# Soft-capped attention with a spectral mix: the second pair's scores of the mixing slots move next to the first pair's

## The chip, the cores and the metric

The kernel runs on one core of one Trainium2 chip. The metric is the device time of one execution in microseconds (us). Three runs of the kernel before took 862.06, 863.33 and 863.35 us; their median is 863.33 us. One further execution was profiled.

## What is computed

Eight batches, twelve heads, 448 tokens, head size 64; the attention's output feeds a mix over tokens and over 768 features.

```python
scores = scale * q @ k.T                    # per batch and head
scores = cap * tanh(scores / cap)
attn = exp(scores - max); attn = attn / (sum(attn) + 1e-09)
x = (attn @ v) as [8, 448, 768]
theta = x @ w_theta
zr, zi = x * cos(theta), x * sin(theta)
y = einsum('ts,bsd->btd', w_tok_r, zr) + einsum('ts,bsd->btd', w_tok_i, zi)
u = x + y
out = u + maximum(u @ w_ch, 0)
```

## The kernel before

Heads are taken in pairs (64 + 64 rows fill the 128 partitions), and two pairs at a time make a **slot** `s`: 24 slots, three for each batch. A slot makes the transposed scores of its two pairs, tanh and exp on them, and the column sums; the product with `v` (`V0`, `W`, `Vr`), the reciprocal (`I`) and the scaling (`N`, two multiplications on VectorE) of slot `s` come during slot `s + 1`. The queries and keys are split into a high and a low float32r part (`prep_q`, `prep_k`), so a score block takes three matmuls, each as two matmuls of 64 rows side by side. The 448 keys are three blocks of 128 and a rest of 64.

From slot 4 on, each slot also carries one third of the spectral mix of an earlier batch, and that is its part, `(s - 4) % 3`: part 0 makes theta (`T`, turns `y`, reduction `d`, sine and cosine `sc`, product with x `r`, a 32 x 32 transpose `f`, and a carry `D` that moves the blocks by 16 DMAs), part 1 is the **mixing slot** (slots 5, 8, 11, 14, 17, 20, 23), part 2 makes the channel product (`C`, `c`, splits `u` and `X`). In a mixing slot the six features j = 0 to 5 (of 128 columns each) are mixed over the 896 token rows (cosine and sine). A feature comes in two halves, a (four blocks, 512 wide in the rows of the profile) and b (three blocks, 384 wide). `h2a` is the high part of feature 2's half a: a cast on ScalarE (L647). `l2a` is its low part: a subtraction on VectorE (L654). `M2a` is its matmuls (three for each block, L664 to L666; the third of each block reads the low part). `m2` adds the result to x on VectorE (L672). Two features share one carried tile: `f0`, `f1` and `D0` bring features 0 and 1, `f2`, `f3` and `D1` features 2 and 3, `f4`, `f5`, `D2` and `E2` features 4 and 5. `E2` is the last four of the sixteen pieces, issued on ScalarE's queue (L633).

What each engine does, and in which order, is written out by hand: `PARTS` has one string of words for each part, `OTHER` the strings of single slots, and `run` issues the words from left to right. Each engine executes its own share in that order, and so do the queues that issue DMAs. The word `S0` makes two key blocks of the first pair, `S1` the third block and both pairs' rests, `S2` and `S3` the second pair's; `t0` to `t3` are their tanhs and `e0` to `e3` their exps (on ScalarE), `a0a` ... `a1b` add the exps of a pair on VectorE (L435, L438, L439), `F0` and `F1` fold the sums (transpose L446, reduce L447), and `Rb` has TensorE sum the folds (L487), which it takes in order. `Pa1`, `Pb1` split query and key of the slot's second pair, `Pa0` and `Pb0` those of the next slot's first.

`once(s)` is true for slots whose scores come in two visits of TensorE: `S0` by itself, and `S1`, `S2`, `S3` one after the other. In these slots `S2` writes two banks of the pool `psM`, `S3` writes the score bank that held the rests and two more banks of `psM`. There are four `psM` banks, and the mix, theta and channel sums take them too. Before, `once` holds for parts 0 and 2 from slot 9 on:

```python
    ONCE = (0, 2)
    def once(s):
        return s > LEAD + 3 and s < NS and (s - LEAD) % NP2 in ONCE
```

Of the kernel before, what the change touches and what calls it, by code (L numbers as in the profile page):

```python
# [12 lines left out]
F32 = mybir.dt.float32  # L13
# [15 lines left out]
LEAD = 4  # L29
# [53 lines left out]
def softcap_attn_then_spectral_mix(ctx, tc, qk2, v, cap, w_theta, w_tok, w_ch, outT):  # L83
# [200 lines left out]
            state["scores"] = state["scope"].enter_context(tc.tile_pool(name=f"ps{general}{s}", bufs=1, space=bass.MemoryType.PSUM))  # L284

    def once(s):
        return s > LEAD + 3 and s < NS and (s - LEAD) % NP2 in ONCE

    def load_raw(k, part, last=False):
        t = raw[k, part] = small.take([P, S], F32, f"{'qk'[part]}{k}", None, int(part == 0 and once(k // 2) and (k // 2 - LEAD) % NP2 == 2), last)  # L290
        nc.sync.dma_start(t, qk2[k // NP, k % NP, :, part, :])
# [19 lines left out]
            if once(k // 2) and k % 2 and (k // 2 - LEAD) % NP2:  # L311
                Q[k, "rooms"] = [small.take([P, S], F32R, f"k{k}{part}") for part in "hl"]

    def prep_k(k):

        if 2 * WHOLE <= k < 2 * NS:
            t = raw.pop((k, 1))
            if once(k // 2) and k % 2:
                if (k, "rooms") not in Q:
                    Q[k, "rooms"] = [small.take([P, S], F32R, f"k{k}{part}") for part in "hl"]  # L320
                rooms = iter(Q[k, "rooms"])
                Q[k, "k"] = halves(t[:, :REST], [P, REST], lambda shape, dtype, name: next(rooms)[:, :REST], f"k{k}", by_scalar(k))
# [55 lines left out]
    def direct(s):  # L378
        return state["general"] or s < DIRECT

    def tanh(s, n):
        m = len(BURSTS[n])
        if m == 2:
            pp = large.take([P, 2, 2, S], F32, f"p{s}_{n}", EXPS if s < LEAD - 1 else None, s >= LEAD and n != 2)
            users[s, n] = [pp, {0: {"V0"}, 1: {"Vr", "V0"}, 2: {"W"}}[n] | (({"Ra", "Rb"}, {"Ra"}, {"Ra", "Rb"})[n] if direct(s) else set())]
        else:
            pp = wk.tile([P, 1, 2, S], F32, tag="p1", name=f"p{s}_{n}", bufs=1)
        for u, what in enumerate(BURSTS[n]):
            U[s, what] = pp[:, u]
        t, whole = spt.pop((s, n)) if not isinstance(spt[s, n], list) else (spt.pop((s, n)), None)  # L390
# [286 lines left out]
    def chan_out(b, m):  # L677
# [15 lines left out]
    )  # L693
    OTHER = {
# [19 lines left out]
    def pipeline(general):  # L714
        state["general"] = general
        nc.scalar.activation(curve, quarter, AF.Tanh)
        def run(s, b, word):
# [9 lines left out]
                scores(s + 1, 0)  # L727
            elif name in ("S", "t", "e"):
                if live:
                    {"S": scores, "t": tanh, "e": exp}[name](s, i)  # L730
            elif not name:
                if live:
                    add(s, i, half)
# [33 lines left out]
            elif name == "q":  # L767
                for part in range(2):
                    if s + 1 < WHOLE or s + 1 == WHOLE and (i, part) != (1, 1):
                        load_raw(2 * s + 2 + i, part)  # L770
            elif word == "Pa1":
                prep_q(2 * s + 1)
            elif word == "Pb1":
                prep_k(2 * s + 1)
# [94 lines left out]
```

## Time and profile before

| what | us |
|---|---|
| median of 3 runs (862.06 to 863.35) | 863.33 |
| the profiled execution, its own time | 861.66 |
| span of the profiled execution | 859.5 |
| TensorE matmuls busy | 852.2 (99%) |
| VectorE busy | 714.9 (83%) |
| ScalarE busy | 582.4 (68%) |
| GpSimd busy | 111.1 (13%) |

The span runs from the first to the last instruction that the profile shows; 2.16 us of the execution lie around it. The granted clock of TensorE is 0.999 of full speed. Busy time of TensorE counts overlapping matmuls once and their ends are modelled, so steps between the starts of matmuls tell more than their durations. VectorE and ScalarE start an instruction up to 0.1 us before the row of the one ahead of it ends, so chains there are added up from start to start.

### The profile page before, as it was taken

Reading aid. Unit: us, or ns where it says so; the run is one execution under the profiler, and the core shown is the slowest. Engines: PE = TensorE matmul, PEld = TensorE weight load, DVE = VectorE, ACT = ScalarE, POOL = GpSimd, SP = SyncE. Lnnn points to the kernel's source line nnn. Section 1 sums busy time; section 2 is a strip of 40 time slices with the busy share of each in tenths; the row PEclk is TensorE's granted clock in tenths of the full one; section 3 lists DMA queues with packets and bytes.
Section 4 is the critical chain, followed back from the end, with each engine's and each line's share of the span. In section 5 each row is a group of like instructions: output and inputs, shape, how many; then the busy total and the mean of one; then the engine's idle time right before and its main releaser. Section 6 shows DMA issues by size and latency. Waiting matters only on the chain.

```text
span 859.5 us, 13319 instructions
## 1 busy us (share of the span) xinstructions
PE 852.2 (99%) x4756; PEld 645.8 (75%) x4756; DVE 714.9 (83%) x1153; ACT 582.4 (68%) x734; POOL 111.1 (13%) x232
## 2 busy tenths in 40 slices
PE   9999999999999999999999999999999999999997
PEld 4335676867878778778787787797787977879996
DVE  5988989999799798989979798897879979776741
ACT  7898987769783777827968479655778377824420
POOL 1121242201300031000310013000130003100300
PEclk9999999999999999999999999999999999999999
DMA  8686275731522334331523314133152332311501
GB/s 315 189 304 229 75 239 196 249 108 53 152 73 90 96 88 121 87 104 54 139 78 97 125 49 132 50 119 118 44 140 68 101 101 74 99 43 31 143 13 56
DMA packets 51884, 99.74 MB, mean 116 GB/s; under 512 B 11232, under 2 KB 42592, under 8 KB 51808
## 3 DMA queue, kind: packets, MB, share of 16 engines
q1 hardware_dynamic: 38304, 58.13, 21.7%
q0 software_dynamic: 9184, 29.20, 11.0%
q10 hardware_dynamic: 4320, 11.47, 4.5%
q8 instruction: 39, 0.64, 0.3%
q14 instruction: 37, 0.30, 0.1%
HBM read 54.72 MB, written 11.01 MB: 76 GB/s over the span
## 4 chain that ended last, share of the span: by engine, by line
PE 96%; ACT 2%; DMA 1%; SPq 1%; issue 0%; POOL 0%; DVE 0%; ACTq 0%; POOLq 0%
PE s L376 13%; PE a L473 13%; PE mx L664 8%; PE mx L666 7%; PE mx L665 7%; PE th L563 7%; PE ch L563 7%; PE ch L564 7%; PE ch L565 7%; PE th L564 7%; PE th L565 7%; PE a L467 2%; PE r L508 2%; PE s_u L376 1%; ACT p L396 1%; DMA t<-g_row 1%
## 5 line engine op out<-in xcount | busy, mean ns | idle before, releaser
L633 POOL DMA_DIRECT2D t<-g_row x148 | 73.5, 504 | 538.1 <-ACT z L587 381.1
L664 PE MATMUL mx<-wtk_h,zh 128*128 128x448 f32 x336 | 125.1, 372 | 0.0
L666 PE MATMUL mx<-wtk_h,zl 128*128 128x448 f32 x336 | 123.7, 368 | 0.1
L665 PE MATMUL mx<-wtk_l,zh 128*128 128x448 f32 x336 | 123.5, 367 | 0.0
L415 ACT ACTIVATE p<-p,singles 128x1792 f32<-128x1792 f32 (+1 forms) x76 | 117.7, 1556 | 1.7 <-PE a L473 0.6
L563 PE MATMUL th<-xs,wth_h 128*128 128x448 f32 x288 | 106.2, 369 | 0.0
L563 PE MATMUL ch<-us,wch_h 128*128 128x448 f32 x288 | 106.0, 368 | 0.0
L564 PE MATMUL ch<-us,wch_h 128*128 128x448 f32 x288 | 105.6, 367 | 0.0
L565 PE MATMUL ch<-us,wch_l 128*128 128x448 f32 x288 | 105.6, 367 | 0.0
L564 PE MATMUL th<-xs,wth_h 128*128 128x448 f32 x288 | 105.5, 366 | 0.0
L565 PE MATMUL th<-xs,wth_l 128*128 128x448 f32 x288 | 105.5, 366 | 0.0
L402 ACT ACTIVATE p<-s,singles 128x896 f32<-128x896 f32 x48 | 45.7, 1004 | 85.4 <-PE s L376 85.3
L473 PE MATMUL a<-p,v 128*64 128x448 f32 x492 | 101.8, 545 | 0.0
L654 DVE TENSOR_TENSOR zl<-t,zh 128x512 fp32r<-128x512 f32 x88 | 52.9, 618 | 28.7 <-ACT zh L647 23.7
L473 PEld LDWEIGHTS a<-p,v 128*64 128x64 f32 x492 | 32.9, 137 | 56.5 <-issue 51.7
L647 ACT CAST zh<-t 128x512 fp32r<-128x512 f32 x88 | 46.9, 563 | 37.3 <-DMA t<-g_row 12.9
L664 PEld LDWEIGHTS mx<-wtk_h,zh 128*128 128x128 f32 x336 | 63.1, 188 | 11.6 <-issue 5.0
L666 PEld LDWEIGHTS mx<-wtk_h,zl 128*128 128x128 f32 x336 | 63.1, 188 | 6.5 <-DVE zl L654 0.9
L665 PEld LDWEIGHTS mx<-wtk_l,zh 128*128 128x128 f32 x336 | 63.2, 188 | 5.5
L563 PEld LDWEIGHTS th<-xs,wth_h 128*128 128x128 f32 x288 | 54.1, 188 | 8.1 <-issue 1.6
L563 PEld LDWEIGHTS ch<-us,wch_h 128*128 128x128 f32 x288 | 54.1, 188 | 6.9 <-ACT p L399 1.6
L564 PEld LDWEIGHTS th<-xs,wth_h 128*128 128x128 f32 x288 | 54.0, 188 | 4.9 <-DVE xs L556 0.2
(673 smaller groups left out, 1690.3 us busy)
## 6 DMA issues: line engine op xcount, KB each, us to landing
v<-in_v ACTq DMA_DIRECT2D x22, 448.0 KB, 3.9
bc<-ri SPq DMA_DIRECT2D x76, 112.0 KB, 2.9
t<-g_row SPq DMA_DIRECT2D x148, 56.0 KB, 2.4
t<-g_row POOLq DMA_DIRECT2D x148, 56.0 KB, 2.3
out_dram<-x SPq DMA_DIRECT2D x36, 224.0 KB, 1.9
q<-in_qk SPq DMA_DIRECT2D x35, 224.0 KB, 2.9
k<-in_qk SPq DMA_DIRECT2D x34, 224.0 KB, 3.8
x_row<-in_qk SPq DMA_DIRECT2D x27, 224.0 KB, 3.4
```

The costliest lines, as they stand in the source:

```text
L376: nc.tensor.matmul(out[h][rows, :S], kk[half], qq[half], start=m == 0, stop=m == len(products) - 1)
L415: nc.scalar.activation(pp, pp, AF.Exp, scale=cap_sb)
L473: nc.tensor.matmul(acc_of["a", s, i][h * D : (h + 1) * D, :S], vt[s][:, 6 * i + 3 * h + c, :], U[s, (i, c)][:, h, :], start=first and c == ...
L563: nc.tensor.matmul(acc[:, :S], wh[:, j, ms], t[:, 0, :], start=j == 0, stop=False)
L564: nc.tensor.matmul(acc[:, :S], wh[:, j, ms], t[:, 1, :], start=False, stop=False)
L565: nc.tensor.matmul(acc[:, :S], wl[:, j, ms], t[:, 0, :], start=False, stop=j == NJ - 1)
L633: queue.dma_start(t[32 * m : 32 * m + 32, d * S : (d + 1) * S], f[32 * d : 32 * d + 32, m * S : (m + 1) * S])
L647: nc.scalar.copy(zh.rearrange("p c (d x) -> p c d x", x=32), tokens(b, j)[:, c0:c1])
L654: nc.vector.tensor_tensor(zl, tokens(b, j)[:, c0:c1], zh.bitcast(F32), op=ALU.subtract)
L664: nc.tensor.matmul(acc[:, :S], zh, wtk_h[:, c, :], start=c == 0, stop=False)
L665: nc.tensor.matmul(acc[:, :S], zh, wtk_l[:, c, :], start=False, stop=False)
L666: nc.tensor.matmul(acc[:, :S], zl, wtk_h[:, c, :], start=False, stop=c == NC2 - 1)
```

## The change

`once` now holds for every slot from 9 to 23, so the mixing slots 11, 14, 17, 20 and 23 make their scores in two visits as well. The strings of part 0 and part 1 are written anew for that; slot 8 keeps the old string of a mixing slot under a name of its own, with an `N` more. The core of the diff:

```diff
-ONCE = (0, 2)
...
     def once(s):
-        return s > LEAD + 3 and s < NS and (s - LEAD) % NP2 in ONCE
+        return LEAD + 4 < s < NS
...
-    def tanh(s, n):
+    def tanh(s, n, part=""):
...
         if once(s) and n == 3:
-            nc.scalar.activation(pp[:, 0], spt.pop((s, "u"))[:, :, :S], AF.Tanh, scale=qscale)
-            for h, each in enumerate(t):
-                nc.scalar.activation(U[s, (1, 1)][:, h], each[:, :S], AF.Tanh, scale=qscale)
+            if part != "a":
+                nc.scalar.activation(pp[:, 0], spt.pop((s, "u"))[:, :, :S], AF.Tanh, scale=qscale)
+            if part != "b":
+                for h, each in enumerate(spt.pop((s, n))):
+                    nc.scalar.activation(U[s, (1, 1)][:, h], each[:, :S], AF.Tanh, scale=qscale)
+            return
...
-        if j < 4 or not 0 < b < B - 1:
+        if j < 4 or not 0 < b < B - 1 or once(LEAD + NP2 * b + 1):
             nc.vector.tensor_scalar(y.bitcast(I32), n.bitcast(I32), 0x7FFFFFFF, None, op0=ALU.bitwise_and)
...
     PARTS = (
-        "S0 t0 V0 e0 Pa1 W Ra Rb Vr cV0 S1 Pb1 cV1 t1 S2 S3 v w0 q0 I w1 a0a Pa0 Pb0 q1 t2 e1 a0b T0 y0 t3 N d0 e2 F0 T1 y1 e3 d1 a1a sc0 a1b T2 y2 r0 r1 f0 f1 D0 T3 y3 d2"
-        " d3 T4 y4 sc1 F1 T5 y5 r2 r3 f2 f3 D1",
-        "S0 t0 V0 h0a l0a h0b l0b W h1a Ra Rb Vr cV0 cV1 d4 d5 l1a Pa1 S1 t1 sc2 Pb1 q0 M0a h1b sc2b l1b I M0b r4 r5 h2a m0 l2a f4 f5 D2 M1a e0 M1b e1 h2b l2b w1 h3a E2"
-        " S2 S3 m1 M2a l3a M2b h3b l3b t3 a0a M3a h4a l4a M3b h4b l4b t2 a0b m2 v q1 M4a h5a e2 l5a m3 M4b"
-        " h5b l5b Pa0 Pb0 F0 e3 a1a M5a m4 M5b a1b w3 m5 F1",
+        "S0 t0 V0 e0 Pa1 Pb1* W Ra Rb Vr cV0 S1 cV1 t1 S2 S3 v w0 q0 I w1 a0a Pa0 Pb0 q1 t2 Pa3 e1 a0b T0 y0 t3 N d0 e2 F0 Pb3* T1 y1 e3 d1 a1a sc0 a1b T2 y2 r0 r1 f0 f1 D0 T3 y3 d2"
+        " d3 T4 y4 d4 sc1 F1 T5 y5 r2 r3",
+        "S0 t0 V0 f2 W Ra Rb f3 D1 h0a Vr cV0 S1 cV1 t1a S2 S3 t2 l0a h0b d5 l0b I h1a l1a sc2b M0a h1b M0b r4 l1b r5 h2a M1a t3a f4 l2a h2b f5 D2 m0 l2b M1b h3a w1 E2 t1b"
+        " N M2a h3b l3a l3b m1 M2b e0 t3b a0a M3a h4a l4a e1 M3b h4b l4b h5a l5a a0b e2 M4a m2 F0 e3 m3 M4b h5b l5b v q1 Pa0 Pb0 a1a M5a m4 M5b a1b w3 m5 F1",
```

A tanh word with a or b after it does half of its work; `Pa3` and `Pb3*` split query and key of the next slot's second pair; a star keeps the raw key until `S1`. Part 2 and the string after the last slot lose an `N-` (the scaling of the slot before the last), which the mixing slot now does by its own `N`. In slot 8 the `N` stands between `m3` and `M4b`. `cV1`, the copy of the second pair's product, goes from ScalarE to VectorE in the mixing slots, and so does the absolute value of theta's last two features.

**TensorE, slot 11, from the third block of the first pair on.** `s11_10` is that block, `s11_20` to `s11_31` and `s11_u` are the second pair's, `mx2_0` is feature 0. Before:

```order
L376 MATMUL s11_10_2951<-q22h_2670,k22l_2675 128x448 x2
L376 MATMUL s11_10_2951<-q22l_2671,k22h_2674 128x448 x2
L664 MATMUL mx2_0_2974<-wtk_h_75,zh2_2917 128x448
L665 MATMUL mx2_0_2974<-wtk_l_76,zh2_2917 128x448
L666 MATMUL mx2_0_2974<-wtk_h_75,zl2_2918 128x448
```

and with the change:

```order
L379 MATMUL s11_u_2976<-q23l_2686,k23h_2689 128x448 x2
L379 MATMUL s11_u_2976<-q23h_2685,k23l_2690 128x448 x2
L379 MATMUL s11_30_2974<-q23h_2685,k23h_2689 128x448
L379 MATMUL s11_31_2975<-q23h_2685,k23h_2689 128x448
L379 MATMUL s11_30_2974<-q23l_2686,k23h_2689 128x448
L379 MATMUL s11_31_2975<-q23l_2686,k23h_2689 128x448
L379 MATMUL s11_30_2974<-q23h_2685,k23l_2690 128x448
L379 MATMUL s11_31_2975<-q23h_2685,k23l_2690 128x448
L674 MATMUL mx2_0_3011<-wtk_h_75,zh2_2942 128x448
L675 MATMUL mx2_0_3011<-wtk_l_76,zh2_2942 128x448
L676 MATMUL mx2_0_3011<-wtk_h_75,zl2_2943 128x448
```

The nine pairs of the second pair's scores, which stood between feature 1 and feature 2, now stand ahead of feature 0.

**ScalarE, slot 11, around the four carry DMAs of `E2`.** `zh2` from `t2_1` and `t2_2` are the high parts of features 2, 3 and 4, 5 (512 is half a, 384 half b); an ACTIVATE at L402 or L399 (L411, L401, L398 in the change) is a tanh, one at L415 (L425) an exp, and `g_row_79` holds the exps' second tile. Before:

```order
L415 ACTIVATE p11_0_2907<-p11_0_2907,singles_64 128x1792
L415 ACTIVATE g_row_79<-g_row_79,singles_64 128x1792
L647 CAST zh2_2917<-t2_1_2876 128x384
L647 CAST zh2_2917<-t2_1_2876 128x512
L633 DMA t2_2_3018<-g_row_79 32x448 x4
L647 CAST zh2_2917<-t2_1_2876 128x384
L399 ACTIVATE p11_3_3110<-s11_30_3076,singles_64 128x448
L399 ACTIVATE p11_3_3110<-s11_31_3077,singles_64 128x448
L647 CAST zh2_2917<-t2_2_3018 128x512
L647 CAST zh2_2917<-t2_2_3018 128x384
```

and with the change:

```order
L657 CAST zh2_2942<-t2_1_2925 128x384
L657 CAST zh2_2942<-t2_1_2925 128x512
L643 DMA t2_2_3058<-g_row_79 32x448 x4
L411 ACTIVATE g_row_79<-s11_10_2918,singles_64 128x896
L657 CAST zh2_2942<-t2_1_2925 128x384
L425 ACTIVATE p11_0_2900<-p11_0_2900,singles_64 128x1792
L398 ACTIVATE p11_3_3051<-s11_u_2976,singles_64 128x896
L657 CAST zh2_2942<-t2_2_3058 128x512
L425 ACTIVATE g_row_79<-g_row_79,singles_64 128x1792
L657 CAST zh2_2942<-t2_2_3058 128x384
L657 CAST zh2_2942<-t2_2_3058 128x512
```

The two exps `e0` and `e1` stood ahead of the four DMAs and now stand behind them, with a tanh ahead of the first.

**VectorE, slot 11, the low parts of features 4 and 5** (`zl2` from `t2_2`), with the additions and the fold of the first pair's exps (`ps11_0`, `ft11_0`) and the sums of features 2 and 3 (`mx2_2`, `mx2_3`). Before:

```order
L654 TENSOR_TENSOR zl2_2918<-t2_2_3018,zh2_2917 128x512
L654 TENSOR_TENSOR zl2_2918<-t2_2_3018,zh2_2917 128x384
L438 TENSOR_TENSOR ps11_0_3113<-ps11_0_3113,g_row_79 128x896
L439 TENSOR_TENSOR ps11_0_3113<-ps11_0_3113,g_row_79 64x896
L672 TENSOR_TENSOR x7_0_1979<-mx2_2_3085,x7_0_1979 128x448
L654 TENSOR_TENSOR zl2_2918<-t2_2_3018,zh2_2917 128x512
L672 TENSOR_TENSOR x7_1_1981<-mx2_3_3115,x7_1_1981 128x448
L654 TENSOR_TENSOR zl2_2918<-t2_2_3018,zh2_2917 128x384
L301 TENSOR_TENSOR q24l_3178<-x_row_80,q24h_3177 128x448
L301 TENSOR_TENSOR k24l_3182<-k24_2972,k24h_3181 128x384
L327 COPY r24_3185<-k24_2972 128x64
L446 STREAM_TRANSPOSE ft11_0_3189<-ps11_0_3113 128x896
```

and with the change:

```order
L664 TENSOR_TENSOR zl2_2943<-t2_2_3058,zh2_2942 128x512
L664 TENSOR_TENSOR zl2_2943<-t2_2_3058,zh2_2942 128x384
L664 TENSOR_TENSOR zl2_2943<-t2_2_3058,zh2_2942 128x512
L448 TENSOR_TENSOR ps11_0_3118<-ps11_0_3118,g_row_79 128x896
L449 TENSOR_TENSOR ps11_0_3118<-ps11_0_3118,g_row_79 64x896
L682 TENSOR_TENSOR x7_0_1979<-mx2_2_3090,x7_0_1979 128x448
L456 STREAM_TRANSPOSE ft11_0_3166<-ps11_0_3118 128x896
L457 TENSOR_REDUCE folds_78<-ft11_0_3166 128x28
L682 TENSOR_TENSOR x7_1_1981<-mx2_3_3120,x7_1_1981 128x448
L664 TENSOR_TENSOR zl2_2943<-t2_2_3058,zh2_2942 128x384
L299 TENSOR_TENSOR q24l_3185<-x_row_80,q24h_3184 128x448
```

Feature 5's half a moved ahead of the addition; its half b, which stood ahead of the fold, now stands behind it.

## Rows read from the trace of the kernel before

**Rows 1.** The page, chain that ended last: shares of the span by engine

```profile
PE 96%; ACT 2%; DMA 1%; SPq 1%; issue 0%; POOL 0%; DVE 0%; ACTq 0%; POOLq 0%
```

**Rows 2.** Windows: slots 17 and 20, from `S0` to `S0`; length, then busy by engine

```profile
513.99:550.81 36.82, 36.82 (x208) 29.10 (x208) 31.75 (x49) 29.46 (x38) 8.40 (x17) 1.00 0.40 116
616.19:653.51 37.32, 37.26 (x209) 28.91 (x208) 30.44 (x47) 29.46 (x38) 8.53 (x17) 1.00 0.41 115
```

**Rows 3.** Timeline of PE, slot 17: start, duration, engine, line, operation, count

```profile
520.97 0.54 PE L376 MATMUL s<-q,r 64*64 64x448 f32 x1
...
532.97 0.37 PE L376 MATMUL s<-q35l,k35h 64*128 64x448 f32 x2
533.26 0.47 PE L664 MATMUL mx<-wtk_h,zh 128*128 128x448 f32 x1
533.57 0.36 PE L665 MATMUL mx<-wtk_l,zh 128*128 128x448 f32 x1
533.77 0.36 PE L666 MATMUL mx<-wtk_h,zl 128*128 128x448 f32 x1
```

**Rows 4.** Timeline of PE, slot 16 (part 0), its second visit

```profile
488.33 0.54 PE L376 MATMUL s<-q,r 64*64 64x448 f32 x1
...
491.84 0.47 PE L563 MATMUL th<-xs,wth_h 128*128 128x448 f32 x1
```

**Rows 5.** Timeline of ACT and its DMA queue, slot 17; in brackets idle before, releaser

```profile
525.21 1.28 ACT L604 ACT_TABLE_LOAD   x1
526.51 1.05 ACT L604 ACTIVATE z<-z,singles 128x896 f32<-128x896 f32 x1
...
533.70 1.18 ACTq L633 DMA_DIRECT2D t<-g_row  x2
...
534.92 1.26 ACTq L633 DMA_DIRECT2D t<-g_row  x2
536.27 0.51 ACT L647 CAST zh<-t 128x384 fp32r<-128x384 f32 x1 [0.84 <-ACT zh L647]
536.69 1.16 ACT L399 ACTIVATE p<-s,singles 128x448 f32<-128x448 f32 x2
539.74 0.62 ACT L647 CAST zh<-t 128x512 fp32r<-128x512 f32 x1 [1.89 <-PE mx L666]
...
540.67 1.90 ACT L402 ACTIVATE p<-s,singles 128x896 f32<-128x896 f32 x2
542.47 0.61 ACT L647 CAST zh<-t 128x512 fp32r<-128x512 f32 x1
542.98 1.80 ACT L415 ACTIVATE p<-p,singles 128x1792 f32<-128x1792 f32 x1
```

**Rows 6.** Timeline of DVE, slot 17

```profile
528.43 1.09 DVE L609 TENSOR_TENSOR z<-z,x 128x896 f32<-128x896 f32 x1 [0.59 <-ACT z L605]
529.44 1.08 DVE L609 TENSOR_TENSOR z<-z,x_row 128x896 f32<-128x896 f32 x1
...
531.57 2.10 DVE L617 STREAM_TRANSPOSE g_row<-z 128x896 f32<-128x896 f32 x2
...
541.46 1.08 DVE L438 TENSOR_TENSOR ps<-ps,g_row 128x896 f32<-128x896 f32 x1
...
543.59 0.61 DVE L672 TENSOR_TENSOR x<-mx,x 128x448 f32<-128x448 f32 x1
544.12 0.67 DVE L654 TENSOR_TENSOR zl<-t,zh 128x512 fp32r<-128x512 f32 x1
...
545.26 0.54 DVE L654 TENSOR_TENSOR zl<-t,zh 128x384 fp32r<-128x384 f32 x1
...
546.83 1.09 DVE L446 STREAM_TRANSPOSE ft<-ps 128x896 f32<-128x896 f32 x1
```

**Rows 7.** Timeline of DVE, then of PE, start of slot 9, behind slot 8

```profile
248.75 1.09 DVE L447 TENSOR_REDUCE folds<-ft 128x28 f32<-128x896 f32 x1
...
249.66 0.53 PE L487 MATMUL s<-folds,diagonal 128*64 128x28 f32 x4
```

More of the change, by code (lines that the diff above doesn't have):

```diff
@@ L312, in prep_q, with prep_k @@
                 Q[k, "rooms"] = [small.take([P, S], F32R, f"k{k}{part}") for part in "hl"]
-    def prep_k(k):
+    def prep_k(k, early=False):
         if 2 * WHOLE <= k < 2 * NS:
-            t = raw.pop((k, 1))
+            t = raw[k, 1]
             if once(k // 2) and k % 2:
@@ L327, in prep_k @@
                 nc.vector.tensor_copy(Q[k, "r"], t[:, REST:])
-            small.give(t)
+            if early:
+                Q[k, "early"] = True
+            else:
+                small.give(raw.pop((k, 1)))
             if k + 1 < 2 * NS:
@@ L357, in scores @@
                     small.give(raw.pop((k + i, 0)))
+                if Q.pop((k + 1, "early"), False):
+                    small.give(raw.pop((k + 1, 1)))
                 if k + 2 < 2 * NS:
-                    load_raw(k + 2, 0)
-                    load_raw(k + 3, 0)
+                    for i in range(2, 4):
+                        load_raw(k + i, 0, once(s) and (s - LEAD) % NP2 == 2)
     def chunk(s, what, out):
@@ L379, in direct @@
         return state["general"] or s < DIRECT
-    def tanh(s, n):
+    def tanh(s, n, part=""):
         m = len(BURSTS[n])
[L383 to L390, printed above, removed]
-        if once(s) and n == 3:
-            nc.scalar.activation(pp[:, 0], spt.pop((s, "u"))[:, :, :S], AF.Tanh, scale=qscale)
-            for h, each in enumerate(t):
-                nc.scalar.activation(U[s, (1, 1)][:, h], each[:, :S], AF.Tanh, scale=qscale)
-        elif whole is not None:
+        if part != "b":
+            if m == 2:
+                pp = large.take([P, 2, 2, S], F32, f"p{s}_{n}", EXPS if s < LEAD - 1 else None, s >= LEAD and n != 2)
+                users[s, n] = [pp, {0: {"V0"}, 1: {"Vr", "V0"}, 2: {"W"}}[n] | (({"Ra", "Rb"}, {"Ra"}, {"Ra", "Rb"})[n] if direct(s) else set())]
+            else:
+                pp = wk.tile([P, 1, 2, S], F32, tag="p1", name=f"p{s}_{n}", bufs=1)
+            for u, what in enumerate(BURSTS[n]):
+                U[s, what] = pp[:, u]
+            U[s, "t", n] = pp
+        pp = U[s, "t", n]
+        if once(s) and n == 3:
+            if part != "a":
+                nc.scalar.activation(pp[:, 0], spt.pop((s, "u"))[:, :, :S], AF.Tanh, scale=qscale)
+            if part != "b":
+                for h, each in enumerate(spt.pop((s, n))):
+                    nc.scalar.activation(U[s, (1, 1)][:, h], each[:, :S], AF.Tanh, scale=qscale)
+            return
+        t, whole = spt[s, n] if isinstance(spt[s, n], tuple) else (spt[s, n], None)
+        if whole is not None:
             nc.scalar.activation(pp, whole[:, :m, :, :S], AF.Tanh, scale=qscale)
@@ L400, in tanh @@
         else:
-            for u in (1, 0) if n == 1 else range(m):
+            for u in {"a": (1,), "b": (0,)}.get(part, (1, 0) if n == 1 else range(m)):
                 nc.scalar.activation(pp[:, u], t[u][:, :, :S], AF.Tanh, scale=qscale)
-        U[s, "t", n] = pp
+        if part != "a":
+            del spt[s, n]
     def used(s, word):
@@ L476, in av_out @@
     def av_out(s, i):
-        x = small.take([P, S], F32, f"x{s}_{i}")
+        x = small.take([P, S], F32, f"x{s}_{i}", None, int(i == 1 and once(s + 1)))
         (nc.vector.tensor_copy if i and once(s + 1) else nc.scalar.copy)(x, acc_of.pop(("a", s, i))[:, :S])
@@ L705, in softcap_attn_then_spectral_mix @@
         " S2 S3 t2 :1ch4a :2ch4a :*ch4b t3 c1 :0ch4b a0b C2 :*ch5a :1ch4b :2ch4b e2 :0ch5a :*ch5b C3 c2 :1ch5a :2ch5a :0ch5b :1ch5b :2ch5b a1a Pa0 Pb0 q1 N- c3 C4 e3 a1b N c4 X0 X1 X2 X3 C5 X4 X5 c5",
+        LEAD + 4: "S0 t0 V0 h0a l0a h0b l0b W h1a Ra Rb Vr cV0 cV1 d4 d5 l1a Pa1 S1 t1 sc2 Pb1 q0 M0a h1b sc2b l1b I M0b r4 r5 h2a m0 l2a f4 f5 D2 M1a e0 M1b e1 h2b l2b w1 h3a E2"
+        " S2 S3 m1 M2a l3a M2b h3b l3b t3 a0a M3a h4a l4a M3b h4b l4b t2 a0b m2 v q1 M4a h5a e2 l5a m3 N M4b"
+        " h5b l5b Pa0 Pb0 F0 e3 a1a M5a m4 M5b a1b w3 m5 F1",
         LEAD + 3: "S0 t0 V0 e0 W Ra Rb Vr cV0 cV1 v w0 Pa1 I S1 Pb1 q0 t1 w1 a0a e1 T0 y0 a0b d0 N T1 y1 d1 F0 sc0 S2 S3 t2 t3 T2 y2 r0 r1 f0 f1 D0 d2"
         " e2 T3 y3 Pa0 Pb0 q1 e3 d3 a1a a1b F1 sc1 T4 y4 T5 y5 r2 r3 f2 f3 D1",
-        NS: "u0 u1 Vr V0 u2 u3 u4 u5 N- W cV0 cV1 Ra Rb I C0 c0 X0 X1 C1 c1 X2 X3 C2 c2 N X4 X5 T0+ y0+ d0+ T1+ y1+ d1+ sc0+ T2+ r0+ r1+ f0+ f1+ D0+ y2+ d2+ T3+"
+        NS: "u0 u1 Vr V0 u2 u3 u4 u5 W cV0 cV1 Ra Rb I C0 c0 X0 X1 C1 c1 X2 X3 C2 c2 N X4 X5 T0+ y0+ d0+ T1+ y1+ d1+ sc0+ T2+ r0+ r1+ f0+ f1+ D0+ y2+ d2+ T3+"
             " y3+ d3+ sc1+ T4+ r2+ r3+ f2+ f3+ y4+ d4+ T5+ D1+ y5+ d5+ h0a+ l0a+ h0b+ l0b+ sc2+ C3 c3 r4+ r5+ f4+ f5+ D2+ C4 h1a+ l1a+ c4 C5 c5",
@@ L729, in run @@
                 if live:
-                    {"S": scores, "t": tanh, "e": exp}[name](s, i)
+                    {"S": scores, "t": tanh, "e": exp}[name](s, i, *word[2:])
             elif not name:
@@ L770, in run @@
                         load_raw(2 * s + 2 + i, part)
[L771 to L774, printed above, removed]
+            elif word in ("Pa1", "Pa3"):
+                prep_q(2 * s + int(word[2]))
+            elif word in ("Pb1", "Pb1*", "Pb3*"):
+                prep_k(2 * s + int(word[2]), "*" in word)
             elif word == "Pa0":
```

2 rows, old and new, of the table PARTS are left out of this document.

## The prediction

> **What bounds the kernel now.** I read the chain of work that ended last first: TensorE has 96% of it [rows 1], so only what shortens TensorE's list of matmuls, or makes it wait, changes the time. Next the windows: a mixing slot is 36.82 us, all of it TensorE work, with VectorE busy 31.75 and ScalarE 29.46 of it [rows 2]. Neither has much to spare, and each runs its list in order, so the question of this change is whether they hand over a half of a feature late. Then the timelines, slot 17 as the pattern. I count from R, the first matmul of the rests (520.97) [rows 3]; the next slot's `S0` stands at 550.81 [rows 2], R + 29.84.
>
> **What TensorE saves.** Leaving the row-split scores for the mix costs two longer steps: 532.97 to 533.26 is 0.29 and on to 533.57 is 0.31, where 0.20 follows [rows 3]. That is 0.20 for one crossing; I take the crossing into the scores to cost the same. The old mixing slot goes mix, scores, mix between `S1` and its end; the new one has `S1`, `S2`, `S3` in one visit, as slot 16 has, where it lasts from 488.33 to 491.84, 3.51 [rows 4]. One visit less saves two crossings, 0.39 a slot: with no wait the next `S0` would stand at R + 29.45. The same 126 mix matmuls follow.
>
> **What ScalarE and VectorE then have to do.** The last low part is `l5b`. The third of the nine matmuls of `M5b` reads it; six more steps of 0.20 and the step of 0.29 lie behind, so it is wanted 1.5 ahead of `S0`, at R + 27.95. When is it there? The chain, with an instruction of ScalarE starting 0.10 before its predecessor's end (540.67 + 1.90 against 542.47) and one of VectorE 0.08 [rows 5, 6]:
>
> 1. To the second sine's end. Before, it released VectorE at 528.43, R + 7.46 [rows 6]. With the change the table load ahead of the sines waits behind `t2`, which waits for `S2`. Six steps of 0.20 and one of 0.30 ahead of the visit's end at R + 3.51, the last pair of `S2` starts at R + 2.0 and lasts 0.37; two tanhs (1.16), a cast of 384 (0.51) and one of 512 (0.62), less 0.2 of overlap [rows 5], bring the load to about R + 4.5, where it was at R + 4.24 (525.21). So R + 7.75.
> 2. To `f5`'s end, F: `r4` and `r5` 1.0 each, the two transposes 2.1, `l1b` 0.47 and `l2a` 0.6 between them [rows 6]: 5.2, F = R + 12.95. (Before: 531.57 + 2.10 = R + 12.70.)
> 3. The four DMAs of `E2` wait for F (533.70) and end at 536.18; the cast behind them begins at 536.27, after 0.84 idle [rows 5]. So whatever stands behind them starts at F + 2.6. Before, that was one cast and two tanhs; `e0` and `e1` had run ahead. Now seven instructions stand between the DMAs and the end of `h5a`: `t1b` 0.90, `h3b` 0.41, `e0` 1.70, `t3b` 0.90, `h4a` 0.51, `e1` 1.70, `h4b` 0.41, then `h5a` itself 0.61, 7.15 in all: F + 9.75.
> 4. VectorE behind it: `l5a` 0.60, `a0b` 2.13 (541.46 to 543.59), `m2` 0.53, `F0` 2.13 (1.13 from the transpose to the reduce, whose duration is 1.09 [rows 6, 7]), `m3` 0.53, `l5b` 0.54 [rows 6]: 6.46, so F + 16.2, R + 29.2.
>
> That is 1.25 later than wanted, 1.3 with the release: **a wait of 1.3 in each changed mixing slot**, on the low part of feature 5's half b. `S0` follows 1.5 behind `l5b`'s end, with some hundredths for the release: R + 30.75 against R + 29.84, 0.9 longer. In slots 11, 14, 17 and 23 that is 3.6. Slot 20 was longer than slot 17 by 0.50 already [rows 2]; the same chain sets its end, so it pays 0.4.
>
> **The norm in slot 8.** `N` puts two multiplications of 448, as long as `m2` (0.53 each), 1.07, ahead of `M4b`, and VectorE goes on without a gap to `F1`, whose reduce ends at 249.84, while the matmuls that sum it start at 249.66 and the last of the four ends at 250.19 [rows 7]: they already wait. TensorE pays the 1.07. Slot 9 is rid of its `N-` only behind that.
>
> **Edits that I cost at nothing.** The splits `Pa3`, `Pb3*` (about 1.9) and `d4` (about 1.4) fall in part 0, where VectorE has time left before `F1` is wanted. `f2`, `f3` and `D1` follow in the next slot, where they already ran; `f3` now stands behind the sums' release, which delays the eight SP and eight POOL issues of `D1` by about 1.4. `f4` and `h2a` wait for their landing. `f4` ran at 531.57 before [rows 6] and is due 0.3 later now; I give 0 here, and up to 0.5 a slot if the landing is later still. The second copy `cV1` on VectorE (0.53) and the absolute value (0.4 twice a batch) fall into its pauses ahead of `r4` (0.59 idle there [rows 6]). ScalarE's one tanh more is in step 1. Without `N-`, part 2 gives VectorE 1.07 back, which nobody waits for.
>
> **Sum.** 3.6 + 0.4 + 1.07 = 5.1 on the profiled execution's 861.66: 866.7. That execution is 1.67 below the median of the runs; on 863.33 the sum is **868.4**.
>
> **A rule against the rows.** In slot 17 the table load begins at 525.21 and takes 1.28, and the sine begins at 526.51, 0.02 after it [rows 5]. The Trainium skill (ScalarE: Activation LUTs, "What ACT_TABLE_LOAD costs") puts a drain of about 1.38 us behind each load, 2.66 in all. By that rule step 1 and with it `l5b` would come 1.38 later in five slots, 6.9 more, 875.3. The rows show no drain, so the sum goes without it.
>
> **Rivals.**
> - *The carry DMAs do not hold what stands behind them.* If `t1b` could start while the four are issued, up to 2.5 earlier, `l5b` would be there in time and only the saving were left: 4 x 0.39, 0.39 + 0.50 in slot 20, less 1.07 in slot 9: 1.4 faster, 861.9; with the norm hidden as well 860.9. For it: the one cast behind them, at 536.27, could have waited for something else. Against it: it starts 0.09 after the last issue's end, and the row names no other engine that ended its 0.84 of idle time [rows 5]. The point is a wait below 0.4 a slot: then the saving wins.
> - *The carried tile of features 4 and 5 lands late.* `h4a` waits for it. At 539.74 it began after 1.89 idle, F + 6.1, where a matmul is named that had long been done, so a DMA [rows 5]. The new chain wants it at F + 6.5. A landing later by 1.0 pushes `l5b` by up to 0.6, and a late `D1` can add 0.5: five slots by 1 us, 873.4.
> - *The page's drain.* A load that holds ScalarE for 2.66: 875.3. The rows speak against it.
> - *The saving and the wait cancel.* If VectorE reaches `a0b` 0.9 earlier than step 4 has it, the slots stay as long as they were and slot 9's 1.07 is left: 864.
>
> **How the numbers follow.** About 0.2% (1.7 us) is what a measurement of this kernel can tell from no change: 861.6 to 865.1. The forecast has 0.65, the late landing 0.10, the drain 0.02: slower 0.77. The DMAs that hold nothing have 0.15, of which 0.08 with the norm hidden (faster) and 0.07 at 861.9 (same); the draw has 0.08 (same): same 0.15. The range reaches from the gain of 861.9 up to the late landing at 873.4, and leaves out the faster case and what lies above.
>
> **What would show it.** Right: in the changed slots a gap of about 1.3 in the mix ahead of the third matmul of `M5b`, released by the low part's subtraction; the exps `e0` and `e1` behind the four DMAs; the fold's reduce ahead of the last subtraction; mixing slots of about 37.7 from `S0` to `S0`; one visit less in each; and the fold's matmuls of slot 9 waiting a microsecond longer. Wrong: mixing slots of 36.4 with no gap; or a gap ahead of features 2 or 4, which would be the carries' landing.

## The result and the profile after

The changed kernel takes 869.49 us (median of 4 runs, 869.39 to 870.03), the kernel before beside it 863.07 (4 runs, 862.06 to 863.35): ratio 1.0078, 95% interval 1.006 to 1.0095. It is slower: the interval lies above 1. The profiled execution took 869.47, its span is 867.7; before, 861.66 and 859.5. The lines of the code moved with the change: the low part of a half is L664, its cast L657, the matmuls of the mix L674 to L676, the carry L643.

The page first, the chain that ended last; the line to put beside it is [rows 1].

```profile
PE 76%; DVE 9%; DMA 4%; ACT 4%; issue 3%; SPq 2%; POOL 1%; ACTq 0%; DVEq 0%
```

TensorE's share went from 96% to 76%: other engines now release it. Where, the windows show: slot 9 before, then slots 9, 17 and 20 with the change (length, then busy time of PE, PEld, DVE, ACT and POOL; clock, DMA share, GB/s).

```profile
243.68:276.57 32.89, 32.89 (x189) 25.96 (x189) 32.11 (x50) 19.00 (x26) 0.00 (x0) 1.00 0.28 84
243.88:277.95 34.07, 33.01 (x189) 25.95 (x189) 32.02 (x49) 18.99 (x26) 0.00 (x0) 1.00 0.28 84
518.07:556.10 38.03, 36.68 (x208) 28.96 (x208) 31.17 (x48) 28.32 (x37) 8.13 (x17) 1.00 0.34 99
621.60:660.61 39.01, 37.27 (x208) 28.95 (x208) 31.07 (x48) 28.44 (x37) 8.40 (x17) 1.00 0.33 97
```

Beside [rows 2], slot 17 is 1.21 longer and slot 20 1.69. From the first `S0` matmul of a slot to that of the next, slot 11 is 1.29 longer (38.36 against 37.07), slot 14 1.39, slot 9 1.18 (34.07 against 32.89); what follows the `S0` of slot 23 is 1.2 longer. That is 8.0 of the 8.2 by which the span grew. The other slots are as long as before within 0.2.

The timeline of PE at the end of slot 17 (start, duration, engine, line, operation, count; in brackets the idle time before and its releaser):

```profile
554.47 0.47 PE L676 MATMUL mx<-wtk_h,zl 128*128 128x448 f32 x1 [1.32 <-DVE zl L664]
554.78 0.36 PE L674 MATMUL mx<-wtk_h,zh 128*128 128x448 f32 x1
554.98 0.36 PE L675 MATMUL mx<-wtk_l,zh 128*128 128x448 f32 x1
...
556.10 0.47 PE L379 MATMUL s<-q36h,k36h 64*128 64x448 f32 x2
```

This is the third matmul of `M5b`, released by `l5b`. It starts 1.69 after the one ahead of it, in place of 0.20: a wait of 1.5. The same place costs 1.55 in slot 11, 1.69 in slot 14, 1.69 in slot 20 and 1.21 in slot 23. Note that the matmul behind the waiting one follows after 0.31, not 0.20.

The timeline of ACT and its DMA queue in the same slot; [rows 5] is what answers to it. F, the end of `f5`'s transpose, is 537.90.

```profile
536.97 1.03 ACT L657 CAST zh<-t 128x384 fp32r<-128x384 f32 x2
537.93 2.80 ACTq L643 DMA_DIRECT2D t<-g_row  x4
540.78 1.01 ACT L411 ACTIVATE g_row<-s,singles 128x896 f32<-128x896 f32 x1 [2.78 <-DMA t<-g_row]
541.69 0.50 ACT L657 CAST zh<-t 128x384 fp32r<-128x384 f32 x1
542.09 1.79 ACT L425 ACTIVATE p<-p,singles 128x1792 f32<-128x1792 f32 x1
543.79 0.99 ACT L398 ACTIVATE p<-s_u,singles 128x896 f32<-128x896 f32 x1
544.67 0.61 ACT L657 CAST zh<-t 128x512 fp32r<-128x512 f32 x1
545.18 1.79 ACT L425 ACTIVATE g_row<-g_row,singles 128x1792 f32<-128x1792 f32 x1
546.88 1.02 ACT L657 CAST zh<-t 128x384 fp32r<-128x384 f32 x2
```

The seven activations of the prediction's step 3 stand there one behind the other: `t1b`, `h3b`, `e0`, `t3b`, `h4a` (544.67), `e1`, then `h4b` and `h5a` in one row that ends at 547.90, F + 10.0. VectorE goes on from there:

```profile
547.41 1.22 DVE L664 TENSOR_TENSOR zl<-t,zh 128x384 fp32r<-128x384 f32 x2 [1.40 <-ACT zh L657]
548.54 1.08 DVE L448 TENSOR_TENSOR ps<-ps,g_row 128x896 f32<-128x896 f32 x1
...
551.20 1.09 DVE L456 STREAM_TRANSPOSE ft<-ps 128x896 f32<-128x896 f32 x1
...
553.86 0.55 DVE L664 TENSOR_TENSOR zl<-t,zh 128x384 fp32r<-128x384 f32 x1
...
560.88 1.08 DVE L457 TENSOR_REDUCE folds<-ft 128x28 f32<-128x896 f32 x1
```

`l4b` and `l5a`, `a0b`, `m2`, `F0`, `m3`, `l5b`: it ends at 554.41, 0.06 ahead of the matmul that waited. From 547.41 to 561.96 there is no bracket in any row: VectorE runs without a pause until `F1` has ended, and the next slot's second fold matmuls stand at 562.1. They have 0.1 to spare.

### The profile page after: what moved, and what is told of

It reads as the page before. It is cut to its first block, busy times and chain, and to the rows that moved or that the text cites. A ratio compares the mean times of both kernels' runs of the same rounds, so it can differ in the third digit from the quotient of the medians.

```text
span 867.7 us, 13306 instructions
## 1 busy us (share of the span) xinstructions
PE 852.4 (98%) x4756; PEld 645.3 (74%) x4756; DVE 722.0 (83%) x1168; ACT 577.8 (67%) x729; POOL 110.7 (13%) x232
## 4 chain that ended last, share of the span: by engine, by line
PE 76%; DVE 9%; DMA 4%; ACT 4%; issue 3%; SPq 2%; POOL 1%; ACTq 0%; DVEq 0%
PE a L483 11%; PE s L379 10%; PE th L573 7%; PE ch L573 7%; PE ch L575 7%; PE th L575 7%; PE th L574 7%; PE ch L574 7%; PE mx L676 3%; DMA t<-g_row 3%; PE mx L674 3%; PE mx L675 3%; PE a L477 2%; ACT zh L657 1%; SPq L643 1%
## 5 line engine op out<-in xcount | busy, mean ns | idle before, releaser
L643 POOL DMA_DIRECT2D t<-g_row x148 | 73.0, 500 | 545.6 <-ACT z L597 310.1
L676 PE MATMUL mx<-wtk_h,zl 128*128 128x448 f32 x336 | 124.0, 369 | 7.1 <-DVE zl L664 6.8
L674 PE MATMUL mx<-wtk_h,zh 128*128 128x448 f32 x336 | 124.4, 370 | 0.2 <-ACT zh L657 0.2
L425 ACT ACTIVATE p<-p,singles 128x1792 f32<-128x1792 f32 (+1 forms) x76 | 117.1, 1555 | 1.6 <-PE a L483 0.6
L411 ACT ACTIVATE p<-s,singles 128x896 f32<-128x896 f32 x38 | 36.2, 1005 | 89.5 <-PE s L379 89.4
L664 DVE TENSOR_TENSOR zl<-t,zh 128x512 fp32r<-128x512 f32 x88 | 53.2, 615 | 28.9 <-ACT zh L657 27.9
L676 PEld LDWEIGHTS mx<-wtk_h,zl 128*128 128x128 f32 x336 | 63.1, 188 | 16.0 <-DVE zl L664 10.8
L674 PEld LDWEIGHTS mx<-wtk_h,zh 128*128 128x128 f32 x336 | 63.1, 188 | 10.7 <-issue 3.5
L657 ACT CAST zh<-t 128x512 fp32r<-128x512 f32 x88 | 47.6, 562 | 21.3 <-PE mx L675 11.1
```

The lines of the kernel that those rows point to most:

```text
L425: nc.scalar.activation(pp, pp, AF.Exp, scale=cap_sb)
L643: queue.dma_start(t[32 * m : 32 * m + 32, d * S : (d + 1) * S], f[32 * d : 32 * d + 32, m * S : (m + 1) * S])
L657: nc.scalar.copy(zh.rearrange("p c (d x) -> p c d x", x=32), tokens(b, j)[:, c0:c1])
L664: nc.vector.tensor_tensor(zl, tokens(b, j)[:, c0:c1], zh.bitcast(F32), op=ALU.subtract)
L674: nc.tensor.matmul(acc[:, :S], zh, wtk_h[:, c, :], start=c == 0, stop=False)
L676: nc.tensor.matmul(acc[:, :S], zl, wtk_h[:, c, :], start=False, stop=c == NC2 - 1)
```

## The experiments

Each was run beside the kernel before on the same chip, five or more times; ratios are to that kernel, so the changed kernel's 1.0078 is the number to compare with. All work on the changed kernel's text; the words are those of part 1, if nothing else is said. F is the end of `f5`'s transpose in each run.

| run | us | ratio (95%) |
|---|---|---|
| E2 on SP's queue | 878.68 | 1.0189 (1.0175 to 1.0203) |
| norm back in slot 9 | 868.48 | 1.0069 (1.0055 to 1.0082) |
| fold late | 869.41 | 1.0076 (1.0062 to 1.0089) |
| t1b ahead of E2 | 868.99 | 1.0076 (1.0062 to 1.009) |
| e1 behind h5a | 864.68 | 1.0026 (1.0017 to 1.0035) |
| both of these | 863.33 | 1.0013 (1.0004 to 1.0022) |
| both, e0 between the DMAs | 862.34 | 0.9997 (0.9988 to 1.0006) |
| that, norm back, splits moved | 860.42 | 0.9973 (0.9962 to 0.9983) |
| that, splits not moved | 860.97 | 0.9979 (0.997 to 0.9988) |

**The fold back behind the splits.**

```diff
-M4a m2 F0 e3 m3 M4b h5b l5b v q1 Pa0 Pb0 a1a
+M4a m2 e3 m3 M4b h5b l5b v q1 Pa0 Pb0 F0 a1a
```

> F0 goes back behind Pb0, where it stood before the change, so l5b comes 2.1 earlier. Rival (only the order of F0 and l5b is at fault): the waits ahead of M5b's third matmul go, 1.5 in each of five slots, and nothing else waits: 862. Theory (VectorE comes late as a whole: from l5a to the end of F1 its list runs without a pause, and F1 ends 0.1 ahead of the next slot's second fold matmuls): the waits at M5b go, and waits of about 1.4 appear at the second fold matmuls of slots 12, 15, 18, 21: 868 to 869.5.

868 to 869.5 was the theory's number, and it is what came. The waits at `M5b` are gone, and the next slot waits instead. The timeline of PE, start of slot 18:

```profile
562.94 0.30 PE L497 MATMUL s<-folds,diagonal 128*64 128x28 f32 x2 [1.00 <-DVE folds L457]
```

and the windows of slots 17 and 18:

```profile
518.98:555.71 36.73, 36.73 (x208) 29.21 (x207) 29.87 (x47) 28.32 (x37) 8.14 (x17) 1.00 0.36 104
555.71:589.76 34.05, 33.05 (x189) 25.95 (x188) 33.27 (x51) 18.99 (x26) 0.00 (x0) 1.00 0.29 89
```

Slot 17 is 1.30 shorter than with the change, and slot 18 1.30 longer; slots 12, 15 and 21 are 34.3 to 34.6 long, 32.6 to 32.8 with the change. So the place of the fold only chooses which matmul waits. What is late is VectorE's list as a whole, and it has to start earlier.

**The carry DMAs on another queue.**

```diff
-            piece(b, i, 3, d, nc.scalar)
+            piece(b, i, 3, d, nc.sync)
```

> The four carry DMAs of E2 go to SP's queue; ScalarE's order stays otherwise. Theory (the issues hold ScalarE): t1b starts within 0.2 of f5's end, where it started 2.9 behind it; h4a then starts at the landing, about F + 6.1, so h5a ends near F + 9.3 (10.0 with the change) and the wait ahead of M5b's third matmul falls from 1.5 to about 0.9: 866. If SP lands the four earlier by 1, the wait is gone: 862. Rival (the idle time ahead of t1b has another cause, and the issues hold nothing): t1b, h5a and the wait stay as they are, 869.5.

Half a hit and a clear miss. The timeline of ACT, then of SP's queue, in slot 17 (F is 542.45):

```profile
542.77 1.03 ACT L411 ACTIVATE g_row<-s,singles 128x896 f32<-128x896 f32 x1
...
545.77 1.01 ACT L398 ACTIVATE p<-s_u,singles 128x896 f32<-128x896 f32 x1
550.59 0.62 ACT L657 CAST zh<-t 128x512 fp32r<-128x512 f32 x1 [3.81 <-PE mx L676]
...
542.52 6.28 SPq L643 DMA_DIRECT2D t<-g_row  x10
```

`t1b` starts at F + 0.3 and not at F + 2.9: the four issues do hold what stands behind them. But SP now makes ten issues in a row, 6.28 for all, and the last piece is issued up to 548.80. `h4a` starts at F + 8.1 (F + 6.8 with the change). The matmul that the row names had long been done, so it is the landing: the trace has the last of the sixteen pieces down at F + 7.7, with the change at F + 6.0. The whole chain is later, and `M4a` waits too: 9 us lost. In slot 20 TensorE stands idle for 3.2 ahead of `M4a`, and its granted clock falls to half, 1.2 in place of 2.4 GHz, for 6.8 us (the windows ahead of the fall and in it):

```profile
651.00:657.60 6.60, 4.00 (x20) 3.40 (x19) 0.92 (x1) 0.40 (x2) 0.07 (x1) 1.00 0.29 73
657.60:664.40 6.80, 6.20 (x17) 5.38 (x18) 4.78 (x7) 6.80 (x9) 0.00 (x0) 0.50 0.20 67
```

The mix's matmuls step at 0.37 there, and the next `S0` follows `l5b`'s end by 2.55 where the other slots have 1.7, so some 0.9 of what this execution lost is the clock's. The landing that I had taken as given moves with the way in which the sixteen issues are shared out among three queues.

**t1b ahead of the carry DMAs, and e1 behind h5a.** Both together first:

```diff
-h3a w1 E2 t1b N ... h4a l4a e1 M3b h4b l4b h5a l5a a0b e2 M4a m2 F0 e3 m3 M4b h5b l5b
+h3a t1b w1 E2 N ... h4a l4a M3b h4b l4b h5a l5a e1 M4a m2 a0b e2 e3 m3 M4b h5b F0 l5b
```

> ScalarE's list: t1b ahead of the four carry DMAs, in the time it has free until f5's end; e1 behind h5a. VectorE's list: m2 and m3 ahead of a0b and F0, so that no sum waits behind e1. TensorE's list is the same. Theory (the chain from the carry DMAs to l5b is what is late): between the DMAs' end and h5a stand h3b, e0, t3b, h4a, h4b only, h5a ends at F + 7.3 (10.0), l5b at about R + 27.2, F1 about 2 earlier against R; all five waits go, slots of 36.5, 861.9. Rival (the landing of the carried tile sets h4a): h4a starts no earlier than now, a wait of 0.5 or more is left in each slot, 865 or above.

Then each alone. The first half:

> One half of the first reordering alone: t1b goes ahead of the four carry DMAs, all else as with the change. Theory (the tile that these DMAs carry lands at about F + 6.6, so h4a cannot use time gained ahead of it): t1b is done by F, h3b starts 0.9 earlier, but h4a only 0.2 earlier, and everything behind it too: the wait at M5b stays at 1.3 of 1.5, 868.5. Rival (the hold in front of t1b is what sets l5b): all that follows comes 0.9 earlier, the wait falls to 0.6, 865.

The second half:

> The other half alone: e1 goes behind h5a, and m2 and m3 ahead of a0b and F0; t1b stays behind the carry DMAs. Theory (what counts is what stands between the landing and h5a): h4a starts where it did, F + 6.8, h5a ends at F + 8.4 in place of F + 10.0, a0b starts at e1's end, F + 10.1 in place of F + 10.6, l5b comes 0.7 to 1.0 earlier, as in the run with both, less 0.2 a slot: 864 to 865. Rival (the hold in front of t1b is what sets l5b): a0b only waits for e1 in place of h5a, 868.5 to 869.5.

Together they bring 863.33, 6 less than the change, though 1.4 short of the 861.9 expected: `h4a` starts 0.1 to 0.4 earlier, so the rival's ground holds only in part, but a wait of about 0.5, the rival's size, is left at `M5b`: `a0b` now waits for `e1`, which ends at F + 9.9 in slot 17. Alone, `t1b` brings almost nothing (1.0076) and `e1` brings most (1.0026); both came as the theory of the landing has it. Where `h4a` starts and `l5b` ends in slot 14, counted from F, is read from the timelines:

| run | h4a starts | h5a ends | l5b ends |
|---|---|---|---|
| the change | 6.96 | 10.19 | 16.71 |
| t1b ahead of E2 | 6.99 | 10.23 | 16.74 |
| e1 behind h5a | 6.78 | 8.32 | 15.40 |
| both | 6.55 | 8.17 | 15.25 |

With `t1b` out of the way `h3b` starts 0.86 earlier in slot 14, but `h4a` no earlier: it waits for the carried tile, whose last piece lands at F + 6.3 with the change and at F + 6.4 here, 0.6 ahead of `h4a` in both. In slot 17 the last piece lands at F + 6.0 and F + 5.9; there `h4a` does come 0.5 earlier, and the wait falls by 0.4. So ahead of `h4a` the hold and the landing end together, within a few tenths, and time freed there is worth little. Behind it, what stands between `h4a` and `h5a` does delay `l5b`: without `e1` there, `h5a` ends 1.9 earlier in slot 14 and 1.3 in slot 17, and `l5b` 1.3 and 0.7 earlier, the rest being lost because `a0b` then waits for `e1`. `m2` and `m3` changed places in the same run; what they bring by themselves was not tried.

**e0 between the carry DMAs.** The order with both, and `E2` issued in two pairs with `e0` between them; `e1` goes ahead of `h4a`, into the time in which ScalarE waits for the landing.

```diff
-h3a t1b w1 E2 N M2a h3b l3a l3b m1 M2b e0 t3b a0a M3a ... h5a l5a e1 M4a
+h3a t1b w1 E2a e0 E2b N M2a h3b l3a l3b m1 M2b t3b e1 a0a M3a ... h5a l5a M4a
...
-        for d in range(4):
+        for d in {"": (0, 1, 2, 3), "a": (0, 1), "b": (2, 3)}[part]:
             piece(b, i, 3, d, nc.scalar)
```

> As the run with t1b ahead of E2, and in addition e0 stands between the second and the third of the four carry DMAs, and e1 ahead of h4a. Theory (the issues hold what stands behind them, but are made while the activation ahead of them still runs): e0 starts behind the second issue, the last two are issued beside it, h3b starts no later than F + 3.0, e0 ends at F + 3.1 (5.1), e1 ahead of the landing at F + 6.6; h5a ends near F + 8.1 as now, but a0b does not wait for e1 any more, so F0 and l5b come about 0.9 earlier and the 0.5 left at M5b's third matmul goes in slots 11, 14, 17 and 23: 861 to 861.5. Rival (an issue waits until the exp ahead of it has ended): the third issue starts at the exp's end, F + 3.0, the carried tile lands about 1 to 1.5 later, M4a waits about 1: 866 or more.

862.34, some 1 above what was expected. The waits at `M5b` are gone in slots 11, 14 and 20 and 0.2 is left in slot 17, but `M4a` waits 0.3 in slot 14 and 0.65 in slot 20, where `h4a` starts at F + 7.2 and F + 8.1. The landing sets those: the last piece is down at F + 6.6 and F + 7.7.

**The norm and the next splits.** First the norm alone, moved back on the changed kernel's text:

```diff
-e2 l5a m3 N M4b          (slot 8)
+e2 l5a m3 M4b
-a0b e1 t3 C0             (slot 9)
+a0b e1 t3 N- C0
```

> N leaves slot 8 and N- comes back in slot 9, as before the change; all else stays. Theory: VectorE has no pause from M4b to F1 in slot 8, so the second fold matmuls of slot 9 wait 1.06 less and slot 9 is 33.0 long in place of 34.1: 868.4. Rival (the lengthening of slot 9 comes from the second visit's new start in slot 11, or N- costs as much where it returns): 869.5.

Slot 9 is 33.04 long in place of 34.07. No other slot is shorter by more than 0.15, and slots 14 and 20 are 0.4 and 0.2 longer. The median fell by 1.0 and the ratio by 0.0009, which is 0.8 us, and the intervals of the two ratios overlap: it is the trace that shows what the norm costs. The timeline of PE has the four fold matmuls in one row again, without a wait:

```profile
249.69 0.54 PE L497 MATMUL s<-folds,diagonal 128*64 128x28 f32 x4
```

where the changed kernel has

```profile
249.85 0.25 PE L497 MATMUL s<-folds,diagonal 128*64 128x28 f32 x2
251.16 0.30 PE L497 MATMUL s<-folds,diagonal 128*64 128x28 f32 x2 [1.06 <-DVE folds L457]
```

Then, on the order with `e0` between the DMAs, three moves together: the norm back in slot 9, the next slot's splits in VectorE's pause ahead of the landing, and, which the expectation's words do not say, `l5b` ahead of the fold:

```diff
-t3b e1 a0a M3a ... h5a l5a M4a ... h5b F0 l5b v q1 Pa0 Pb0 a1a
+t3b e1 a0a Pa0 M3a ... h5a l5a Pb0 M4a ... h5b l5b F0 v q1 a1a
```

> As that, with slot 8's norm back in slot 9, l5b ahead of nothing new, and the next slot's splits Pa0, Pb0 put ahead of h4a and behind l5a, where ScalarE and VectorE wait for the landing. Theory: no wait at M5b and none at the next slot's fold matmuls; slots 11, 14, 17 of 36.82 less 0.39 for the visit saved, 36.4; slot 9 of 33.0; 860, which is below the kernel before. Rival (the visit saves nothing, the step ahead of S0's pairs being paid elsewhere): slots of 36.8 without a wait, 861.8.

> As the run before it in this call but with the splits at their old place. Theory (VectorE as a whole is what is late next): F1 ends 1.1 later than with the splits moved, within 0.3 of the next slot's second fold matmuls; waits there of up to 0.3 in four slots: 860 to 861.5. Rival (ScalarE's chain to h5a alone decides): same time as with the splits moved.

860.42 with the splits moved: faster than the kernel before by 0.27% (0.17% to 0.38%). Slot 17 has no wait left:

```profile
512.85:549.34 36.49, 36.49 (x208) 29.12 (x207) 31.73 (x49) 28.50 (x37) 8.24 (x17) 1.00 0.38 110
```

It is 0.33 shorter than in [rows 2], 0.39 was expected for the visit saved, and the rival had 36.8. Slot 11 is 0.38 shorter than before. In slot 17 `l5b` ends at F + 13.4. The chain that ended last is TensorE's again:

```profile
PE 97%; ACT 1%; DMA 0%; POOL 0%; issue 0%; DVE 0%; ACTq 0%; POOLq 0%
```

What is left is the landing: in slot 20 `h4a` starts at F + 7.7 and `M4a` waits 0.8 for it. The run without the splits moved shows a wait of 0.3 at the fold matmuls of slot 15 and next to none in slots 12 and 18, and its time, 860.97, is not told apart from 860.42. So moving the splits is not shown to matter. Of the 1.9 that the three moves bring together the norm has about 1.0, by its run alone; what `l5b` ahead of the fold brings was not tried by itself.

## Why the prediction was right, and where its steps were not

The forecast of 868.4 stands against 869.49, and the case was the forecast's: `l5b` late, a wait ahead of the third matmul of `M5b`, slot 9 paying for the norm. Its terms were too small, though: they add up to 5.1, and the two traces have 8.0. By its steps, in slot 17, where R is 525.03:

- **The saving.** 0.39 a slot was predicted; where no wait hides it, in the 860.42 run, it is 0.33 in slot 17 and 0.38 in slot 11.
- **Step 1**, the second sine's end: R + 7.75 predicted, R + 7.67 in the rows below. The load takes 1.28 and the sine starts 0.02 behind its end, so the rival of the drain falls. The Trainium skill (ScalarE: Activation LUTs, "What ACT_TABLE_LOAD costs") puts a drain of about 1.38 us on top of the load; this trace shows none, neither behind the load nor ahead of it, where the cast before ends at 529.5.

```profile
529.51 1.28 ACT L614 ACT_TABLE_LOAD   x1
530.81 1.04 ACT L614 ACTIVATE z<-z,singles 128x896 f32<-128x896 f32 x1
531.76 0.94 ACT L615 ACTIVATE z<-z 128x896 f32<-128x896 f32 x1
```

- **Step 2**, F: R + 12.95 predicted, R + 12.87 measured.
- **Step 3.** `t1b` at F + 2.6 predicted, F + 2.9 measured; `h5a`'s end at F + 9.75, measured F + 10.0. That the issues hold what stands behind them was shown by taking them away. But the step named only half of the cause: the carried tile lands at the time at which the chain reaches `h4a`, and without the hold in front of `t1b` little changes. That `e1` stands between `h4a` and `h5a` is what makes `l5b` late; putting it behind `h5a`, with `m2` and `m3` ahead of the sums, gave most of it back (1.0026 in place of 1.0078).
- **Step 4**, VectorE from `h5a` to `l5b`: 6.46 predicted, 547.90 to 554.41 is 6.51. `l5b` was there at R + 29.38, not R + 29.2, and was wanted at R + 27.95 as predicted: a wait of 1.49, not 1.3. That R + 27.95 came out to the hundredth is luck: `M4a` waited 0.3 for `l4a`, and shorter steps between the mix's matmuls (last section) gave 0.3 back.
- **`S0` behind it.** I let it follow 1.55 behind `l5b`'s end; it follows 1.69 behind, since the matmul behind one that waited comes after 0.31 in place of 0.20. So the slot is 1.21 longer in place of 0.9. Four such slots cost 5.1, where the sum has 3.6: **this term was undersized**, by the hold's 0.3, by that 0.1, and in slots 11 and 14 by an `h5a` that ends another 0.35 and 0.2 later (F + 10.34 and F + 10.19). The small waits for `l4a` cost nothing here: VectorE's rows behind `h5a` have no pause, so `l5b` does not move with them.
- **Slot 20.** The sum has 0.4, the trace 1.69. I took the 0.5 by which the slot was already longer as part of the same wait. It is not: there `h4a` waits for the landing (0.88 idle, starting at F + 7.8, where slot 17 has F + 6.8), the matmuls of `M4a` wait for it as before, and all that follows on ScalarE and VectorE is 1.0 later, so the wait at `M5b` comes on top. The rival of the late landing had this mechanism; it came true in one slot of five. It could have been read ahead of the change: in the trace of before, `h4a` starts at F + 7.5 in slot 20 and at F + 6.1 in slot 17. With the change:

```profile
649.19 0.62 ACT L657 CAST zh<-t 128x512 fp32r<-128x512 f32 x1 [0.88 <-DMA t<-g_row]
```

- **The norm.** 1.07 predicted; the fold matmuls wait 1.06, and slot 9 is 1.03 shorter with the norm back.
- **Edits at nothing.** The slots of parts 0 and 2, except slot 9, are as long as they were, within about 0.2. None of these edits was taken back by itself.

The medians differ by 6.4, less than the 8.0 of the traces: the profiled execution of before lay 1.67 below its median, as the prediction said, and that of the change lies at its own. So it is in part luck that 868.4 came within 1.1 of the result: a sum of 5.1 that was 2.9 too small for the traces is only 1.3 too small for the medians. The rival that the DMAs do not hold fell with `t1b` at F + 0.3 when they were gone; that saving and wait cancel fell with the waits themselves.

## What to carry to other kernels

When work is moved ahead on the bound engine, follow the next value that it wants back through the other engines, and ask of each station both what stands in front of it in its queue and when its data lands: taking away the earlier of the two is worth little (1.0076 against 1.0078 here). An operation that nobody wants soon, such as an exp, is best put into the wait ahead of a landing; behind it, this one's 1.7 cost 0.7 to 1.3 in the two slots read. Where VectorE's list had no pause, moving one fold in it only chose which matmul waits.

## What the runs showed of the hardware that I had not expected

**A DMA issue runs beside the activation ahead of it.** In the 860.42 run, slot 17, the timeline of ACT and its queue:

```profile
533.03 1.02 ACT L411 ACTIVATE g_row<-s,singles 128x896 f32<-128x896 f32 x1
533.34 0.60 ACTq L643 DMA_DIRECT2D t<-g_row  x1
533.99 1.80 ACT L425 ACTIVATE p<-p,singles 128x1792 f32<-128x1792 f32 x1
534.01 1.56 ACTq L643 DMA_DIRECT2D t<-g_row  x2
535.69 0.49 ACT L658 CAST zh<-t 128x384 fp32r<-128x384 f32 x1
```

The last two issues start 0.02 behind the exp's start and are done 0.2 before its end. Issues hold the activations behind them, but not the other way round: `t1b` and `e0`, 2.8 in all, fit into the time that four issues take.

**The step between the mix's matmuls has two values.** From start to start it is 0.2000 or 0.2067 over long stretches, at a granted clock of 1.00 in both. In the same run the windows of the 126 matmuls of slots 14 and 17 (rows of the mix alone) are:

```profile
421.77:447.48 25.71, 25.70 (x126) 23.46 (x126) 2.43 (x4) 1.00 0.44 128
523.38:549.34 25.96, 25.96 (x126) 23.55 (x126) 2.59 (x5) 1.00 0.42 124
```

Slot 14 is shorter although one of its matmuls waits 0.2: 121 of its steps are of the short kind, in slot 17 only 41. In the changed kernel's slot 17, 89 steps are short, before 42: 0.3 given back. What chooses between them was not tried; a slot's length says nothing below some 0.8 without a look at these steps.

**A late landing with a packet on an instruction queue.** In the changed kernel's slot 20, the view of the DMA queues from F to `h4a` (queue, packets, MB, share of 16 engines) has

```profile
q8 instruction: 1, 0.02, 1.0%
```

and slot 17 has no such line; the carried tile's last piece lands at F + 7.4 in slot 20 and at F + 6.0 in slot 17. Slot 14 has one on another queue, of 0.01 MB, and lands at F + 6.3. The view of 646.10 to 648.40, in 40 slices by where a packet starts, has

```profile
GB/s 410 218 187 187 250 125 218 63 0 0 0 0 0 0 0 0 0 0 0 0 0 0 0 31 0 0 31 0 0 62 0 0 0 0 0 0 31 31 0 0
q8 instruction: 1, 0.02, 3.5%
```

The packet takes 1.29 (3.5% of 16 engines), from 646.15 to 647.44 by its record. No other packet starts from 646.6 on until 647.42, when the last ones of the tile follow one by one. It is so in every trace with `E2` on ScalarE's queue, the kernel before among them: slot 20 has such a packet on q8 while the tile is under way and its last piece lands at F + 7.2 to F + 7.8; slot 17 has none, and it is F + 5.7 to F + 6.2. So the packet very likely delays the tile; no run moved or removed it.
